# Fused clustered attention and channel mix: per-head transposes with long load runs, later weight loads, a later cluster step, and mix pieces kept for the end

## The chip, the cores and the metric

One core of one Trainium2 chip. Times are device microseconds of one execution. The span of a trace (first to last instruction) is about 2 us shorter than the execution's time. Engines: PE is TensorE (PEld its weight loads), DVE VectorE, ACT ScalarE, POOL GpSimd, SP the queue that issues most transfers.

## The reference, cut to what matters

```python
# q, k, v: (4 batches, 8 heads, 768 tokens, 64); 16 centroids per head
q_assign = argmax(q_n . c_n)   # cluster of each query, of each key
k_assign = argmax(k_n . c_n)
scores = where(q_assign == k_assign, scale * q @ k.T, -1e9)
attn_out = softmax(scores) @ v
# channel mix on x = attn_out as (4, 768, 512)
xk = mu_k*x + (1-mu_k)*x_prev ; xr likewise
out = sigmoid(xr @ w_r) * (max(xk @ w_k, 0)**2 @ w_v)
```

Of the kernel before, what the change touches and what calls it, by code (L numbers as in the profile page):

```python
# [8 lines left out]
F32 = mybir.dt.float32  # L9
# [7 lines left out]
def kernel(  # L17
# [24 lines left out]
    NG = 4  # L42
    GW = 2 * S // NG
    BIG = 32.0
    NWARM = 10

# [24 lines left out]
    def load_qk(n, eng_q, eng_k):  # L71
        b, j = divmod(n, NP)
        t = nat[n] = loadp.tile([128, 2, NCH, 2, D], F32, name="qk_nat")
        for i, (src, eng) in enumerate(((q, eng_q), (k, eng_k))):
            for h in range(2):
                eng.dma_start(t[:, i, :, h, :],
                              src[b, 2 * j + h].rearrange("(p c) d -> p c d", c=NCH))

    def load_v(n, eng):
        b, j = divmod(n, NP)  # L80
        t = vnat[n] = vloadp.tile([128, 2, NCH, D], F32, name="v_nat")
        for h in range(2):
            eng.dma_start(t[:, h, :, :], v[b, 2 * j + h].rearrange("(p c) d -> p c d", c=NCH))
# [4 lines left out]
    cblk = constp.tile([128, NP, 2 * C], F32)  # L88
# [14 lines left out]
    def krows(t):  # L103
        return slice(0, 64 + C) if t == 0 else slice(0, 128)

    def init_ring(i):
        nc.gpsimd.memset(augs[i][1][0:64, :], 0.0)
        nc.gpsimd.memset(vts[i][:, :, :, D:D + 1], 1.0)
        nc.gpsimd.memset(xts[i][:, 0, 0:1], 0.0)


    qkT = {}

    def trans(n, t3, eng=None):
        if t3 == 0:
            qkT[n] = qktp.tile([128, 2 * S], F32, name="qkT")
        ps = ps_w.tile([128, 512], F32, name="trps", tag="w")
        for i in range(4):
            qk, c = divmod(4 * t3 + i, NCH)
            nc.tensor.matmul(ps[:, i * 128:(i + 1) * 128], nat[n][:, qk, c, :, :], ident,  # L120
                             is_transpose=True, start=(i == 0), stop=(i == 3))
        cs = slice(t3 * 512, (t3 + 1) * 512)
        if eng is nc.scalar:
            nc.scalar.copy(qkT[n][:, cs], ps)
        else:
            nc.vector.tensor_copy(qkT[n][:, cs], ps)  # L126
        for t in range(2):
            rows = slice(64 * t, 64 * t + 64)
            nc.gpsimd.tensor_scalar(augs[n % NR][t][rows, cs], in0=qkT[n][rows, cs],  # L129
                                    scalar1=qk_scale, scalar2=1.0, op0=ALU.mult, op1=ALU.mult)  # L130
# [8 lines left out]
    def aff_mm(n):  # L139
        j = n % NP  # L140
        ps = ps_w.tile([128, GW], F32, name="affps", tag="w")
        for g in range(NG):
            nc.tensor.matmul(ps[32 * g:32 * g + 32, :], cblk[:, j, :], qkT[n][:, g * GW:(g + 1) * GW],  # L143
# [15 lines left out]
    def aff_back(n, engs):  # L159
# [3 lines left out]
        i = 0  # L163
        for t in range(2):
            o = 64 if t == 0 else 0
            for g in range(NG):
                engs[i % len(engs)].dma_start(augs[n % NR][t][o:o + C, g * GW:(g + 1) * GW],
                                              oht[32 * g + C * t:32 * g + C * t + C, :])
                i += 1
# [7 lines left out]
    def scores(t):  # L177
# [3 lines left out]
        rows = krows(tt)  # L181
# [129 lines left out]
    with tc.manual_schedule():  # L311
# [27 lines left out]
        cnt_ps = ps_o.tile([D, NP, 2, C], F32, name="cnt_ps", tag="out2")  # L339
        nc.tensor.transpose(cnt_ps.rearrange("d j t c -> d (j t c)"), cn_sb, ident)  # L340
        nc.vector.tensor_copy(cblk[0:64, :, 0:C], cnt_ps[:, :, 0, :])
        nc.vector.tensor_copy(cblk[64:128, :, C:2 * C], cnt_ps[:, :, 1, :])

        for n in range(2):
# [3 lines left out]
            load_qk(n + 2, nc.sync, nc.sync)  # L348
# [9 lines left out]
        nc.sync.dma_start(mu_k_sb, moe_mu_k.rearrange("(j p) -> p j", p=128))  # L358
        nc.sync.dma_start(mu_r_sb, moe_mu_r.rearrange("(j p) -> p j", p=128))

        def load_wk():
            nc.gpsimd.dma_start(w_k_sb, moe_w_k.rearrange("(j p) f -> p j f", p=128))

        def load_wv():
            nc.gpsimd.dma_start(w_v_sb, moe_w_v.rearrange("(i p) m -> p i m", p=128))

        def load_wr():
            nc.gpsimd.dma_start(w_r_sb, moe_w_r.rearrange("(j p) m -> p j m", p=128))

        def scale_wv():  # L370
            for i in range(NI):
                nc.gpsimd.tensor_scalar(w_v_sb[:, i, :], in0=w_v_sb[:, i, :], scalar1=0.5,
                                        scalar2=1.0, op0=ALU.mult, op1=ALU.mult)

        at(4, load_wk)
        at(16, load_wv)
        at(28, load_wr)
        at(50, scale_wv)

        W = 2 * NCH  # L380
        forced = {}
        for n in range(NPAIR):
            s = n * W
            if n + 2 < NPAIR:
                for t3 in range(3):
                    forced[s + t3] = lambda n=n, t3=t3: trans(n + 2, t3)
                if n + 4 < NPAIR:
                    at(s + 3, load_qk, n + 4, nc.sync, nc.sync)
                forced[s + 3] = lambda n=n: aff_mm(n + 2)
                at(s + 4, aff_max, n + 2)  # L390
                at(s + 5, aff_back, n + 2, [nc.sync])
            if n + 1 < NPAIR:
                at(s + 6, vcast, n + 1)
            if n + 2 < NPAIR:
                at(s + 7, load_v, n + 2, nc.sync)
# [24 lines left out]
        while t < NSTEP + NCH or queue or todo:  # L420
# [6 lines left out]
            elif queue and not (t < NSTEP and (B - 1) * H * NCH + W <= t and t % 6 == 5):  # L427
                queue.pop(0)()
# [31 lines left out]
```

## The kernel before: what the change touches

The mask is made by matmul: each head has a tile `aug` whose rows 0:64 are scaled q or k (transposed, tokens along columns) and whose next 16 rows are the one-hot cluster of each token. One matmul over the rows then gives score plus a large bonus where the clusters agree.

Work goes by pairs of heads (16 pairs) in 12 steps each, 192 steps in all. A step t issues, in this order on TensorE: `scores(t)` (one key chunk against 768 queries), `values(t-6)`, then either a forced task or one piece of the channel mix. ACT takes one exponential of 128x768 per step. Steps s to s+11 of pair n also prepare pair n+2:

```python
def load_qk(n, eng_q, eng_k):                    # 256 B runs, 4 DMAs a pair
    t = nat[n] = loadp.tile([128, 2, NCH, 2, D], F32, name="qk_nat")
    for i, (src, eng) in enumerate(((q, eng_q), (k, eng_k))):
        for h in range(2):
            eng.dma_start(t[:, i, :, h, :], src[b, 2*j + h].rearrange("(p c) d -> p c d", c=NCH))

def trans(n, t3, eng=None):                      # 4 transposes into one PSUM tile
    ...                                          # both heads of one token chunk
    nc.vector.tensor_copy(qkT[n][:, cs], ps)     # DVE: PSUM -> SBUF
    ...                                          # POOL: scaled copies into aug

def aff_mm(n):                                   # "the cluster matmul": 4 column groups of qkT
    for g in range(NG):
        nc.tensor.matmul(ps[32*g:32*g+32, :], cblk[:, j, :], qkT[n][:, g*GW:(g+1)*GW], ...)
    nc.vector.transpose(t1, ps)
# aff_max(n): DVE maximum and one-hot. aff_back(n): DVE transpose to oht, then 8 DMAs aug<-oht

for n in range(NPAIR):
    s = n * W                                    # W = 12
    forced[s + t3] = trans(n + 2, t3)            # t3 = 0, 1, 2
    at(s + 3, load_qk, n + 4, nc.sync, nc.sync)
    forced[s + 3] = aff_mm(n + 2)
    at(s + 4, aff_max, n + 2); at(s + 5, aff_back, n + 2, [nc.sync])
    ...
at(4, load_wk); at(16, load_wv); at(28, load_wr); at(50, scale_wv)     # whole weights, cast to bf16 on the way
while ...:
    scores(t); values(t - NCH)
    if t in forced: forced[t]()
    elif queue and not (t < NSTEP and (B-1)*H*NCH + W <= t and t % 6 == 5):
        queue.pop(0)()                           # one mix piece
```

Each batch puts 30 mix pieces (0.87 us of matmul each) on the queue when its last pair is done.

The softmax here doesn't subtract the row's maximum and nothing guards it: scores larger than these inputs give would overflow.

## Time and profile before

| | before |
|---|---|
| median of 3 runs | 297.51 us (295.93 to 297.65) |
| span of the trace | 296.0 us |
| TensorE busy | 268.1 us, 91% |
| ACT, DVE, POOL busy | 192.8, 179.4, 91.7 us |
| packets under 512 B | 54,368 of 65,661 |

How to read it: a busy share of 91% says that TensorE is the bound on average, and nothing about where the other 28 us are. The views that the prediction shows answer that. One more line of before matters below, from its list of waits (engine, line, what for: us in total, times, longest):

```profile
PEld affps L143 <- DVE qkT L126: 4.5, 16, 0.7
```

The weight loads of the cluster matmul wait for DVE's copy of the transposed block. Three of the 16 waits (1.4 us) belong to the first two pairs, which are prepared before the steps; the other 13 come one to a pair, in 13 of the 14 pairs that the steps prepare, 0.19 or 0.39 us each. It is a small row among some fifty, and I passed over it. One such wait in the timeline of before:

```profile
100.43 0.69 DVE L126 COPY qkT<-trps 128x512 f32<-128x512 f32 x1 [0.15 <-PE trps L120]
...
100.84 1.18 PE L143 MATMUL affps<-qkT,cblk 128*32 128x384 f32 x8
101.17 0.14 PEld L143 LDWEIGHTS affps<-qkT,cblk 128*32 128x32 f32 x4 [0.19 <-DVE qkT L126]
```

Four of the eight weight loads go at 100.84. The other four go at 101.17, just after DVE's copy ends (100.43 + 0.69 = 101.12). TensorE still counts as busy in between, since a recorded matmul of this group lasts 0.51 us.

### The profile page before, as it was taken

To read this page: it belongs to the slowest core of one execution; us is meant where nothing else is said; L and a number is where in the kernel's file an instruction comes from. 1 tells how busy PE (TensorE), PEld (TensorE's weight loads), DVE (VectorE), ACT (ScalarE), POOL (GpSimd) and SP (SyncE) were. 2 spreads that over 40 slices of the span, in tenths; PEclk is the share of its full clock that TensorE was granted. 3 is DMA by queue.
4 is the path that set the end of the run, shared out by engine and by line. 5 is a ranking of instruction groups with operands and counts; after the bars stand their busy time and mean duration, and the time that the engine had idled before them with its cause. 6 is when DMAs were issued, how large, how long until landed. Compare 5 with 4: busy or idle time off the path is not lost.

```text
span 296.0 us, 6426 instructions
## 1 busy us (share of the span) xinstructions
PE 268.1 (91%) x2479; PEld 165.7 (56%) x2507; DVE 179.4 (61%) x337; ACT 192.8 (65%) x268; POOL 91.7 (31%) x154
## 2 busy tenths in 40 slices
PE   6688949999899999999999999989999999869993
PEld 2345636656666656565666656555656555545441
DVE  2764744877967676655867677646766262765321
ACT  3048744877879776776779776666878866606320
POOL 2895607156970413324060605041241000000000
PEclk9979986999999999999999999999999999999999
DMA  8975995936633334435261506231302011110021
GB/s 159 221 164 89 185 188 134 196 76 151 167 107 80 84 87 144 104 132 142 63 151 50 123 15 187 74 112 44 97 6 64 2 71 38 71 38 0 35 108 71
DMA packets 65661, 29.81 MB, mean 101 GB/s; under 512 B 54368, under 2 KB 62048, under 8 KB 65632
## 3 DMA queue, kind: packets, MB, share of 16 engines
q1 hardware_dynamic: 61696, 26.32, 34.9%
q0 software_dynamic: 2096, 2.62, 5.9%
q10 hardware_dynamic: 1840, 0.48, 0.8%
q8 instruction: 20, 0.33, 0.5%
q14 instruction: 9, 0.07, 0.1%
HBM read 24.15 MB, written 6.29 MB: 103 GB/s over the span
## 4 chain that ended last, share of the span: by engine, by line
PE 71%; DVE 9%; ACT 8%; DMA 4%; POOL 3%; issue 3%; SPq 0%; DVEq 0%; ACTq 0%
PE psv L287 14%; PE st L184 10%; PE out L197 9%; PE psk L264 8%; PE trps L120 7%; ACT pt L187 7%; PE psr L276 7%; PE affps L143 5%; PE st L185 5%; PE psk L255 5%; POOL aug L129 3%; DMA aug<-oht 2%; DVE qkT L126 2%; DMA qk_nat<-in_q_dram 2%; PE xtps L217 1%
## 5 line engine op out<-in xcount | busy, mean ns | idle before, releaser
L187 ACT ACTIVATE pt<-st 128x768 bf16<-128x768 f32 x192 | 151.4, 809 | 60.4 <-PE st L185 50.6
L129 POOL TENSOR_SCALAR aug<-qkT 64x512 bf16<-64x512 f32 x96 | 59.4, 619 | 104.8 <-DVE qkT L126 98.9
L184 PE MATMUL st<-aug 80*128 80x512 bf16 (+1 forms) x192 | 74.3, 387 | 7.2 <-DMA aug<-oht 3.9
L197 PEld LDWEIGHTS <-pt 128*128 128x128 bf16 x1152 | 62.7, 98 | 30.3 <-ACT pt L187 4.6
L197 PE MATMUL out<-vt,pt 128*128 128x65 bf16 x1152 | 70.0, 194 | 2.9 <-ACT pt L187 2.3
L185 PE MATMUL st<-aug 80*128 80x256 bf16 (+1 forms) x192 | 52.7, 274 | 0.0
L287 PE MATMUL psv<-w_v_sb,k 128*128 128x512 bf16 x186 | 47.4, 378 | 0.3
L126 DVE COPY qkT<-trps 128x512 f32<-128x512 f32 x47 | 31.6, 702 | 19.3 <-PE trps L120 19.0
L269 ACT ACTIVATE kr<-psk 128x512 bf16<-128x512 f32 x48 | 28.7, 597 | 17.2 <-PE psk L264 13.2
L120 PE MATMUL trps<-ident,qk_nat 128*128 128x128 f32 x192 | 32.3, 294 | 6.0 <-DVE qkT L126 4.6
L291 DVE SCALAR_TENSOR_TENSOR out_sb<-tanh,psv 128x512 f32<-128x512 bf16 x24 | 16.5, 687 | 32.8 <-PE psv L287 26.7
L270 DVE TENSOR_TENSOR k<-kr 128x512 bf16<-128x512 bf16 x48 | 20.9, 436 | 24.7 <-ACT kr L269 24.7
L264 PE MATMUL psk<-xk,w_k_sb 128*128 128x512 bf16 x114 | 31.7, 378 | 3.8 <-DVE xk L240 3.1
L184 PEld LDWEIGHTS <-aug 80*128 80x128 bf16 (+1 forms) x192 | 19.0, 99 | 23.9 <-issue 10.8
L135 POOL CAST vt<-v_nat 128x384 bf16<-128x384 f32 x32 | 17.8, 580 | 31.3 <-DMA v_nat<-in_v_dram 30.5
L120 PEld LDWEIGHTS trps<-ident,qk_nat 128*128 128x128 f32 x192 | 21.6, 148 | 9.6 <-DVE qkT L126 5.9
L185 PEld LDWEIGHTS <-aug 80*128 80x128 bf16 (+1 forms) x192 | 19.1, 99 | 14.0 <-issue 4.4
L287 PEld LDWEIGHTS <-k 128*128 128x128 bf16 x192 | 16.3, 97 | 14.9 <-issue 1.3
L276 PE MATMUL psr<-w_r_sb,xr 128*128 128x512 bf16 x88 | 24.2, 378 | 0.4
L279 ACT ACTIVATE tanh<-psr 128x512 bf16<-128x512 f32 x24 | 14.3, 597 | 14.9 <-PE psr L276 14.7
L143 PE MATMUL affps<-qkT,cblk 128*32 128x384 f32 x128 | 19.7, 509 | 0.7 <-DVE qkT L126 0.5
L146 DVE STREAM_TRANSPOSE t<-affps 128x384 f32<-128x384 f32 x16 | 9.3, 583 | 15.8 <-PE affps L143 15.8
(48 smaller groups left out, 200.4 us busy)
## 6 DMA issues: line engine op xcount, KB each, us to landing
qk_nat<-in_q_dram SPq DMA_DIRECT2D x32, 192.0 KB, 3.9
v_nat<-in_v_dram SPq DMA_DIRECT2D x32, 192.0 KB, 2.7
out_dram<-out_sb SPq DMA_DIRECT2D x24, 256.0 KB, 2.3
qk_nat<-in_k_dram SPq DMA_DIRECT2D x30, 192.0 KB, 4.3
aug<-oht SPq DMA_DIRECT2D x124, 12.0 KB, 1.8
w_k_sb<-in_moe_w_k_dram POOLq DMA_DIRECT2D x1, 1024.0 KB, 9.2
w_v_sb<-in_moe_w_v_dram POOLq DMA_DIRECT2D x1, 1024.0 KB, 10.8
w_r_sb<-in_moe_w_r_dram POOLq DMA_DIRECT2D x1, 512.0 KB, 7.7
```

The source lines that it names most:

```text
L120: nc.tensor.matmul(ps[:, i * 128:(i + 1) * 128], nat[n][:, qk, c, :, :], ident, is_transpose=True, start=(i == 0), stop=(i == 3))
L126: nc.vector.tensor_copy(qkT[n][:, cs], ps)
L129: nc.gpsimd.tensor_scalar(augs[n % NR][t][rows, cs], in0=qkT[n][rows, cs], scalar1=qk_scale, scalar2=1.0, op0=ALU.mult, op1=ALU.mult)
L143: nc.tensor.matmul(ps[32 * g:32 * g + 32, :], cblk[:, j, :], qkT[n][:, g * GW:(g + 1) * GW], start=True, stop=True, tile_position=(0, 32 * g))
L184: nc.tensor.matmul(st[:, 0:512], kc, a[rows, 0:512], start=True, stop=True)
L185: nc.tensor.matmul(st[:, 512:S], kc, a[rows, 512:S], start=True, stop=True)
L187: nc.scalar.activation(pt, st, AF.Exp, bias=-BIG, scale=BIG)
L197: nc.tensor.matmul(o[:, qc, :], pts[bh * NCH + c][:, qc * 128:(qc + 1) * 128], vts[n % NR][:, tt, c, 0:D + 1], start=(c == 0), stop=(c == ...
L264: nc.tensor.matmul(ps, w_k_sb[:, j, ii * 128:(ii + 1) * 128], self.xk[:, j, 0:512], start=(j == 0), stop=(j == NJ - 1))
L269: nc.scalar.activation(kr, src, AF.Relu)
L276: nc.tensor.matmul(ps, self.xr[:, j, sl], w_r_sb[:, j, :], start=(j == 0), stop=(j == NJ - 1))
L287: nc.tensor.matmul(self.psvt, self.k2[:, i, sl], w_v_sb[:, i, :], start=(i == 0), stop=(i == NI - 1))
```

## The change

Its intent: longer load runs and fewer DMAs; no zero rows; transfers moved out of the crowded first 60 us; the cluster step one step away from the transposes that feed it; and some mix pieces kept for the gap at the end. The core of it (not shown: v too comes in one DMA a pair, and its load and its cast go one step later):

```diff
-        t = nat[n] = loadp.tile([128, 2, NCH, 2, D], F32, name="qk_nat")
+        t = nat[n] = loadp.tile([128, 2, 2, NCH * D], F32, name="qk_nat")
...
-            for h in range(2):
-                eng.dma_start(t[:, i, :, h, :], src[b, 2 * j + h].rearrange("(p c) d -> p c d", c=NCH))
+            eng.dma_start(t[:, i, :, :], src[b, 2 * j:2 * j + 2].rearrange("h (p c) d -> p h (c d)", c=NCH))
...
-        nc.gpsimd.memset(augs[i][1][0:64, :], 0.0)
...
-            nc.tensor.matmul(ps[:, ...], nat[n][:, qk, c, :, :], ident, is_transpose=True, ...)
+            nc.tensor.matmul(ps[:, ...], nat[n][:, g // 2, g % 2, c2 * 128:(c2 + 1) * 128], ident, is_transpose=True, ...)
...   # POOL: 8 copies of 64x384 a pair instead of 6 of 64x512; scores over 80 rows for both heads
-        at(4, load_wk) ; at(16, load_wv) ; at(28, load_wr) ; at(50, scale_wv)
+        at(6, load_mu)
+        for i in range(4):
+            at(22 + 6 * i, load_wk, i)
+            at(45 + 3 * i, load_wv, 2 * i)
+        for i in range(2):
+            at(57 + 3 * i, load_wr, 2 * i)
+        for i in range(NI):
+            at(56 + 2 * i, scale_wv, i)
...
-                    at(s + 3, load_qk, n + 4, nc.sync, nc.sync)
-                forced[s + 3] = lambda n=n: aff_mm(n + 2)
-                at(s + 4, aff_max, n + 2)
-                at(s + 5, aff_back, n + 2, [nc.sync])
+                at(s + 3, load_qk, n + 3, nc.sync, nc.sync)
+                forced[s + 4] = lambda n=n: aff_mm(n + 2)
+                at(s + 5, aff_max, n + 2)
+                at(s + 6, aff_back, n + 2, [nc.sync])
...
-            elif queue and not (t < NSTEP and (B - 1) * H * NCH + W <= t and t % 6 == 5):
+            elif queue and not (NSTEP - H * NCH // 2 < t < NSTEP + NCH - 1 and len(queue) <= HOLD):   # HOLD = 5
```

More of the change, by code (lines that the diff above doesn't have):

```diff
@@ L45 @@
     NWARM = 10
+    HOLD = 5
     qk_scale = (1.0 / (D ** 0.5) / BIG) ** 0.5
@@ L72, in load_qk @@
         b, j = divmod(n, NP)
-        t = nat[n] = loadp.tile([128, 2, NCH, 2, D], F32, name="qk_nat")
+        t = nat[n] = loadp.tile([128, 2, 2, NCH * D], F32, name="qk_nat")
         for i, (src, eng) in enumerate(((q, eng_q), (k, eng_k))):
-            for h in range(2):
-                eng.dma_start(t[:, i, :, h, :],
-                              src[b, 2 * j + h].rearrange("(p c) d -> p c d", c=NCH))
+            eng.dma_start(t[:, i, :, :],
+                          src[b, 2 * j:2 * j + 2].rearrange("h (p c) d -> p h (c d)", c=NCH))
     def load_v(n, eng):
@@ L81, in load_v @@
         t = vnat[n] = vloadp.tile([128, 2, NCH, D], F32, name="v_nat")
-        for h in range(2):
-            eng.dma_start(t[:, h, :, :], v[b, 2 * j + h].rearrange("(p c) d -> p c d", c=NCH))
+        eng.dma_start(t.rearrange("p h c d -> p h (c d)"),
+                      v[b, 2 * j:2 * j + 2].rearrange("h (p c) d -> p h (c d)", c=NCH))
     ident = constp.tile([128, 128], F32)
@@ L87 @@
     cn_sb = constp.tile([H * C, D], F32)
-    cblk = constp.tile([128, NP, 2 * C], F32)
+    cblk = constp.tile([128, H, 2, C], F32)
     mu_k_sb = constp.tile([128, NJ], F32)
@@ L101, with augv @@
         xts.append(constp.tile([128, NCH + 1, 128], BF16, name=f"xt{i}"))
-    def krows(t):
-        return slice(0, 64 + C) if t == 0 else slice(0, 128)
     def init_ring(i):
-        nc.gpsimd.memset(augs[i][1][0:64, :], 0.0)
         nc.gpsimd.memset(vts[i][:, :, :, D:D + 1], 1.0)
         nc.gpsimd.memset(xts[i][:, 0, 0:1], 0.0)
+    def augv(n, g):
+        a = augs[n % NR][g % 2].rearrange("p (q c r s) -> p q c r s", q=2, r=2, s=128)
+        return a[:, g // 2, :, :, :]
     qkT = {}
@@ L118, in trans @@
         for i in range(4):
-            qk, c = divmod(4 * t3 + i, NCH)
-            nc.tensor.matmul(ps[:, i * 128:(i + 1) * 128], nat[n][:, qk, c, :, :], ident,
+            g, c2 = divmod(4 * t3 + i, NCH // 2)
+            nc.tensor.matmul(ps[:, i * 128:(i + 1) * 128],
+                             nat[n][:, g // 2, g % 2, c2 * 128:(c2 + 1) * 128], ident,
                              is_transpose=True, start=(i == 0), stop=(i == 3))
@@ L126, in trans @@
             nc.vector.tensor_copy(qkT[n][:, cs], ps)
-        for t in range(2):
-            rows = slice(64 * t, 64 * t + 64)
-            nc.gpsimd.tensor_scalar(augs[n % NR][t][rows, cs], in0=qkT[n][rows, cs],
-                                    scalar1=qk_scale, scalar2=1.0, op0=ALU.mult, op1=ALU.mult)
+        for g in ((0,), (1,), (2, 3))[t3]:
+            for par in range(2):
+                src = qkT[n][64 * par:64 * par + 64, g * GW:(g + 1) * GW]
+                nc.gpsimd.tensor_scalar(augv(n, g)[0:64, :, par, :],
+                                        in0=src.rearrange("p (c s) -> p c s", s=128),
+                                        scalar1=qk_scale, scalar2=1.0, op0=ALU.mult, op1=ALU.mult)
     def vcast(n):
@@ L142, in aff_mm @@
         for g in range(NG):
-            nc.tensor.matmul(ps[32 * g:32 * g + 32, :], cblk[:, j, :], qkT[n][:, g * GW:(g + 1) * GW],
+            nc.tensor.matmul(ps[32 * g:32 * g + 32, :], cblk[:, 2 * j + g % 2, :, :],
+                             qkT[n][:, g * GW:(g + 1) * GW],
                              start=True, stop=True, tile_position=(0, 32 * g))
@@ L162, in aff_back @@
         nc.vector.transpose(oht, ohn)
-        i = 0
-        for t in range(2):
-            o = 64 if t == 0 else 0
-            for g in range(NG):
-                engs[i % len(engs)].dma_start(augs[n % NR][t][o:o + C, g * GW:(g + 1) * GW],
-                                              oht[32 * g + C * t:32 * g + C * t + C, :])
-                i += 1
+        for i, (g, par) in enumerate(((0, 0), (2, 0), (0, 1), (2, 1), (1, 0), (3, 0), (1, 1), (3, 1))):
+            r = 32 * g + C * par
+            engs[i % len(engs)].dma_start(augv(n, g)[64:64 + C, :, par, :],
+                                          oht[r:r + C, :].rearrange("p (c s) -> p c s", s=128))
     NSTEP = B * H * NCH
@@ L180, in scores @@
         a = augs[n % NR][tt]
-        rows = krows(tt)
+        rows = slice(0, 64 + C)
         st = ps_st.tile([128, S], F32, name="st")
@@ L338 @@
         nc.vector.tensor_scalar_mul(cn_sb, in0=cn_sb, scalar1=cn_rnorm)
-        cnt_ps = ps_o.tile([D, NP, 2, C], F32, name="cnt_ps", tag="out2")
-        nc.tensor.transpose(cnt_ps.rearrange("d j t c -> d (j t c)"), cn_sb, ident)
-        nc.vector.tensor_copy(cblk[0:64, :, 0:C], cnt_ps[:, :, 0, :])
-        nc.vector.tensor_copy(cblk[64:128, :, C:2 * C], cnt_ps[:, :, 1, :])
+        cnt_ps = ps_o.tile([D, H, C], F32, name="cnt_ps", tag="out2")
+        nc.tensor.transpose(cnt_ps.rearrange("d h c -> d (h c)"), cn_sb, ident)
+        nc.vector.tensor_copy(cblk[0:64, :, 0, :], cnt_ps)
+        nc.vector.tensor_copy(cblk[64:128, :, 1, :], cnt_ps)
         for n in range(2):
@@ L347 @@
             trans(n, 2)
-            load_qk(n + 2, nc.sync, nc.sync)
+            if n == 0:
+                load_qk(2, nc.sync, nc.sync)
             aff_mm(n)
@@ L357, with load_mu, load_wk, load_wv @@
         init_ring(2)
-        nc.sync.dma_start(mu_k_sb, moe_mu_k.rearrange("(j p) -> p j", p=128))
-        nc.sync.dma_start(mu_r_sb, moe_mu_r.rearrange("(j p) -> p j", p=128))
-        def load_wk():
-            nc.gpsimd.dma_start(w_k_sb, moe_w_k.rearrange("(j p) f -> p j f", p=128))
-        def load_wv():
-            nc.gpsimd.dma_start(w_v_sb, moe_w_v.rearrange("(i p) m -> p i m", p=128))
-        def load_wr():
-            nc.gpsimd.dma_start(w_r_sb, moe_w_r.rearrange("(j p) m -> p j m", p=128))
-        def scale_wv():
-            for i in range(NI):
-                nc.gpsimd.tensor_scalar(w_v_sb[:, i, :], in0=w_v_sb[:, i, :], scalar1=0.5,
-                                        scalar2=1.0, op0=ALU.mult, op1=ALU.mult)
-        at(4, load_wk)
-        at(16, load_wv)
-        at(28, load_wr)
-        at(50, scale_wv)
+        def load_mu():
+            nc.sync.dma_start(mu_k_sb, moe_mu_k.rearrange("(j p) -> p j", p=128))
+            nc.sync.dma_start(mu_r_sb, moe_mu_r.rearrange("(j p) -> p j", p=128))
+        def load_wk(j):
+            nc.gpsimd.dma_start(w_k_sb[:, j, :], moe_w_k.rearrange("(j p) f -> p j f", p=128)[:, j, :])
+        def load_wv(i):
+            nc.gpsimd.dma_start(w_v_sb[:, i:i + 2, :],
+                                moe_w_v.rearrange("(i p) m -> p i m", p=128)[:, i:i + 2, :])
+        def load_wr(j):
+            nc.gpsimd.dma_start(w_r_sb[:, j:j + 2, :],
+                                moe_w_r.rearrange("(j p) m -> p j m", p=128)[:, j:j + 2, :])
+        def scale_wv(i):
+            nc.gpsimd.tensor_scalar(w_v_sb[:, i, :], in0=w_v_sb[:, i, :], scalar1=0.5,
+                                    scalar2=1.0, op0=ALU.mult, op1=ALU.mult)
+        at(6, load_mu)
[6 more added lines that the diff above has]
+            at(56 + 2 * i, scale_wv, i)
         W = 2 * NCH
@@ L383 @@
             s = n * W
+            if n + 3 < NPAIR:
+                at(s + 3, load_qk, n + 3, nc.sync, nc.sync)
             if n + 2 < NPAIR:
@@ L386 @@
                     forced[s + t3] = lambda n=n, t3=t3: trans(n + 2, t3)
-                if n + 4 < NPAIR:
-                    at(s + 3, load_qk, n + 4, nc.sync, nc.sync)
-                forced[s + 3] = lambda n=n: aff_mm(n + 2)
-                at(s + 4, aff_max, n + 2)
-                at(s + 5, aff_back, n + 2, [nc.sync])
+                forced[s + 4] = lambda n=n: aff_mm(n + 2)
+                at(s + 5, aff_max, n + 2)
+                at(s + 6, aff_back, n + 2, [nc.sync])
+                at(s + 8, load_v, n + 2, nc.sync)
             if n + 1 < NPAIR:
-                at(s + 6, vcast, n + 1)
-            if n + 2 < NPAIR:
-                at(s + 7, load_v, n + 2, nc.sync)
+                at(s + 7, vcast, n + 1)
             at(s + W - 1, norm, 2 * n)
```

## The prediction

> **What bounds the kernel now.** I read the views in this order: the page's 40 slices, the table of windows, the chain that ended last, the timeline around its one long transfer, then the chain near the end. First the slices (each digit tenths of a slice of 7.4 us: busy share of TensorE, its granted clock, busy share of the DMA engines):
>
> ```profile
> PE   6688949999899999999999999989999999869993
> ...
> PEclk9979986999999999999999999999999999999999
> DMA  8975995936633334435261506231302011110021
> ```
>
> TensorE is at 9 nearly everywhere. The soft places are the first four slices, slices 6 and 7 (37 to 52 us, a 4 and a clock of 6) and slices 35 and 36 (about 255 to 270 us). The windows table separates these (columns: stretch, its length, busy us and count of PE, PEld, DVE, ACT, POOL, then clock, DMA share, GB/s):
>
> ```profile
> 43.00:60.00 17.00, 16.18 (x159) 11.68 (x160) 10.22 (x18) 11.31 (x15) 6.53 (x12) 0.82 0.80 171
> ...
> 100.90:117.00 16.10, 15.99 (x159) 10.21 (x162) 10.67 (x21) 11.66 (x17) 5.00 (x9) 1.00 0.42 114
> 249.40:265.40 16.00, 12.14 (x131) 7.32 (x131) 9.96 (x19) 6.65 (x9) 0.00 (x0) 1.00 0.13 50
> ```
>
> From 100.9 to 117.0 us one head pair (12 steps with eight pieces of the channel mix) takes 16.1 us with TensorE busy throughout, ACT 11.7, DVE 10.7, POOL 5.0, DMA at 0.42: TensorE-bound. The sum of the chain's own pieces agrees: 12 x (0.22 + 0.11 + 0.19) for scores and values, 8 x 0.87 mix, 3 x 0.47 transposes, 1.10 cluster matmul, 0.34 for the output transpose = 16.05 us. Nothing that shortens loads or moves them can help there. The other two stretches have holes.
>
> The cluster matmul (affps) comes once per pair, so its starts on the chain are a clock for the pairs:
>
> ```profile
> 32.19 1.13 PE affps L143 x6
> ...
> 49.48 0.97 PE affps L143 x8
> ...
> 60.48 1.13 PE affps L143 x6
> ...
> 71.64 1.10 PE affps L143 x6
> ```
>
> Before the mix begins (near 79 us) a pair takes 11.0 and 11.16 us: twelve exponentials of 0.809 us are 9.7, so this phase is bound by ACT, plus the steps in which transposes starve it. But the pair from 32.19 to 49.48 took 17.29 us. What took the time, on the chain:
>
> ```profile
> 35.16 0.59 SPq L167
> ...
> 35.79 7.19 DMA aug<-oht
> ...
> 43.02 0.61 PE st L184
> ```
>
> and in the timeline:
>
> ```profile
> 31.22 3.20 SPq L76 DMA_DIRECT2D qk_nat<-in_k_dram  x2
> 34.52 6.19 SPq L167 DMA_DIRECT2D aug<-oht  x8
> ...
> 43.02 0.61 PE L184 MATMUL st<-aug 80*128 80x512 bf16 x1 [3.92 <-DMA aug<-oht]
> 44.87 0.63 PE L184 MATMUL st<-aug 80*128 80x512 bf16 x1
> 50.91 0.38 PE L184 MATMUL st<-aug 80*128 80x512 bf16 x1
> ```
>
> The one-hot rows of the third pair were ready at about 25.5 us (DVE's transpose to oht runs 24.95 to 25.53), but their eight small copies start issuing only at 34.52: four q and k loads of 768 runs of 256 B each stand before them on SP, from 27.5 on, and they share the engines with the 1 MB w_k load issued at 24.57 (9.2 us to landing; two tiny mu loads took 9.0 and 7.7). The copies then need up to 7.2 us against a median of 1.8. TensorE stands still, and restarts slow: the same 128x512 score matmul takes 0.61 to 0.63 us until about 49 us and 0.38 after. Near the end:
>
> ```profile
> 260.82 0.69 DVE out_sb L291
> ...
> 261.76 0.57 DVE xn L210
> ...
> 264.34 1.03 DVE xk L240
> ...
> 265.41 0.38 PE psk L264
> ```
>
> After the last values matmuls (end 261.5) the last pair's normalise, transpose, shift chain runs through DVE until 265.4 while TensorE has only a transpose and three mix matmuls. From there the last batch's 30 mix pieces run back to back.
>
> **What the Trainium skill says.** "DMA: Bandwidth & Descriptors", section "Specifications", gives 512 B as the least transfer for line rate. The trace agrees: 54,368 of 65,661 packets are under 512 B, and while q and k come in 256 B runs the engines are full at about 215 to 220 GB/s; where the v load (1536 B runs) is in flight at 11 to 12 us they reach 349 to 386. The same page, "Issuing engines are not separate DMA queues", says that all issuing queues share the same 16 engines; the late one-hot copies beside w_k are that. "TensorE: Matmul & The Clock Gate", "Part 1: The HAM clock gate", puts an idle window of about 3.4 us before half clock; the 3.92 us wait and the 0.61 us matmuls after it agree. Its Part 2 ("Step-by-step") says that row count does not matter for a weight load; here 80-row and 128-row loads both take 97 to 101 ns, so cutting the odd head from 128 to 80 rows is worth nothing.
>
> **The change, part by part.**
>
> (1) Load runs of 1536 B, one DMA per pair of heads. Packets of q and k fall from 49,152 to 8,192. At the start, 786 KB (q and k of pair 0) at 220 GB/s is 3.6 us, at 360 GB/s 2.2 us; bulk flow began near 2.7 us, so both are there by about 5.5 us instead of 6.2 (q) and 7.4 (k). The warm-up matmuls and centroid transpose hold TensorE until 5.3 us, so I take 0.8 us of it.
>
> (2) No zeroing of the odd head's upper 64 rows. Three memsets of 1.37 us go. Two are on the early chain: the third runs 18.88 to 20.25 beside the DVE cast to identb, which takes 1.45 us there for 128x128, and a transpose then waits 1.12 us for DVE's copy behind it. I read this as the two engines holding each other up, and take 1.2 us. Start together: 2.0 us.
>
> (3) Weight loads split and later (w_k from step 22, not 4), the pair load one pair shorter ahead. In the early phase SP now issues: pair 1's one-hots from about 17 us (eight at 0.63 us, to 22), two qk loads (to 23.5), mu (to 25.7), then pair 2's one-hots, ready about 24, issued by 31 and landed by 34. They are needed at step 24. With step 3 near 19 us and 0.91 us per step that is 38 us. The stall goes: 17.29 - (11.0 + 11.16)/2 = 6.2 us, cold clock included.
>
> (4) Cluster step one step later. The three transpose steps (0.52 + 0.47 us each) and the cluster step (0.52 + 1.1) were adjacent, 4.6 us of TensorE against 3.2 of exponentials, with two score buffers to bridge. A plain step between them lets ACT keep fed: I estimate 0.1 us per pair over four ACT-bound pairs, 0.4 us. In the TensorE-bound part it is nothing.
>
> (5) The POOL copies are 128 instead of 96, 64x384 instead of 64x512. The mean of 619 ns should become about 510, so 8 x 0.51 against 6 x 0.62: 0.4 us more POOL per pair, at 5.0 of 16 us busy. Beside other work, 0.
>
> (6) Holding five mix pieces for the end. Counting pops: the third batch now finishes 25 pieces by step 182, holds from 183 to 196, and releases five at 197 to 201, into the gap at 261.5 to 265.4. Steps 183 to 191 then run at ACT's pace, 9 x 0.83 = 7.5 us, where TensorE needs 4.7. From after the cluster matmul of the last pair (step 160, 215.0 us) to 265.4 was 50.4 us. New sum: one more step with a piece 1.4, 22 steps at 1.39 plus two output transposes 31.3, held steps 7.5, last exponential 0.9, values 1.15, then three held pieces 2.6, transpose 0.5 and DVE's copy-shift chain 2.55, under which the other two pieces and three mix matmuls fit: 47.9. Gain 2.5 us. It also drops the skips at every sixth step, which had left the chain waiting on an exponential at head boundaries.
>
> Sum: 2.0 + 6.2 + 0.4 + 2.5 = 11.1 us off 297.5, 286.4 us.
>
> **The rivals.** (a) The stall is only moved: another wait takes its place, since weights (5 MB of reads) now land between steps 22 and 60 and DVE's one-hot transposes still wait for eight copy lanes. For it: the DMA share early is 0.92. Against it: the q and k transfers that fill it take about 0.6 of their time now, and the one-hots have about 4 us of slack at step 24 and more later. Then only 2.0 + 2.5 plus half the stall: about 290. (b) POOL becomes the bound in steps 22 to 70, with ten descriptor-writing DMA issues of 0.8 to 0.9 us, eight scalings of 0.87, 13% more copy time, and copies that now write other partitions than they read. If these copies cost double, POOL would need about 10 us of copies and 1.2 of casts per 11 us pair: no gain before 79 us, 293 or worse. The profile has no such shifted POOL copy; I give it 5%. (c) The held pieces give nothing, as starved steps 183 to 191 cost what the end gains: 289. (d) The loads were hidden anyway in the TensorE-bound middle: true, and already counted as zero.
>
> **Range and chances.** The stall is a measured wait and its removal has slack; start and end are sums of small terms, each perhaps 1.5 us wrong. Two rivals (a and c) reach 289 to 292; in the other direction, better pacing might give 3 us more. So 283.5 to 290.5, and 2% faster means below 291.6: 0.91 faster, 0.08 same, 0.01 slower.
>
> **What would show it.** Step 1: first transposes near 5.5 us, few packets under 512 B. Step 2: no long cast to identb. Step 3: cluster matmuls 11 us apart from the first to the fifth pair, no wait of PE for aug<-oht above 1 us, clock at 9 in slice 7, and the pair at 71.64 us now near 63. Step 5: 64x384 POOL copies near 0.51 us. Step 6: a stretch of ACT-paced steps without mix before the last values, and under 1.5 us of TensorE idling after them. The mix-phase pair should stay at 16.1 us; if it changes by more than 0.2 us, my account of the middle is wrong, and nine such pairs would move the total by more than any term here.

## More of the kernel before

The rounds of experiments ran on four chips, each with the kernel before beside it.

## The result, and the profile after

The changed kernel takes 281.67 us (median of 4 runs, 281.53 to 283.43) against 297.58 for the kernel before. The ratio is 0.948, 95% interval 0.942 to 0.954. (Ratios here are the mean time of one kernel's fast runs over that of the other's of the same rounds, so not quite the ratio of the medians.) Faster was right. The size was not: 15.9 us where 11.1 were predicted, and 281.67 lies below the range that began at 283.5.

The slices of the changed kernel, as for before, with the packet line:

```profile
PE   7678998997999999999999999999999999899994
PEclk9999999999999999999999999999999999999999
DMA  7425549669933216135602217135302102020021
...
DMA packets 28141, 29.80 MB, mean 107 GB/s; under 512 B 10704, under 2 KB 24528, under 8 KB 28112
```

The hole at 37 to 52 us is gone and the clock is full everywhere. The cluster matmuls on the chain:

```profile
30.24 0.78 PE affps L148 x8
...
40.59 0.78 PE affps L148 x8
...
51.28 0.78 PE affps L148 x8
...
61.66 0.83 PE affps L148 x8
```

The pairs before the mix now take 10.35, 10.69 and 10.38 us. The stall is gone, as predicted, but these are also faster than the 11.0 and 11.16 of before, and the matmul's own piece fell from about 1.10 to 0.78 us.

A sharper clock than these marks is the start of the exponential of each step, read from the traces (us from the span's start):

| step | before | after | gained so far |
|---|---|---|---|
| 0 | 17.21 | 15.30 | 1.9 |
| 6 | 24.56 | 21.63 | 2.9 |
| 30 | 52.42 | 42.61 | 9.8 |
| 54 | 74.72 | 63.68 | 11.0 |
| 78 | 105.42 | 94.99 | 10.4 |
| 150 | 203.11 | 190.88 | 12.2 |
| 180 | 242.32 | 231.58 | 10.7 |
| end | 296.0 | 279.7 | 16.4 |

(At step 180 the changed kernel has done more of the mix than the old one, hence the dip.) Between steps 6 and 30, where the stall was, it gained 6.9 us, near the 6.2 predicted. But it also gained where I had said nothing or little: 1.2 from 30 to 54, 1.8 from 78 to 150, and 4.2 after step 150, where I had 2.5. In the mix phase the cluster matmul's stretch of the chain shows what changed. Before:

```profile
100.72 0.19 PE out L197 x6
100.91 1.10 PE affps L143 x6
102.01 0.32 PE st L184
```

After:

```profile
107.76 0.19 PE out L200 x6
107.95 0.78 PE affps L148 x8
108.74 0.32 PE st L187
```

From the end of the values matmuls to the next scores it is 1.10 us before and 0.79 after, for eight matmul records each time (before, two of them are not on the chain). The list of waits agrees; what was 4.5 us, 16 times, is now 1.4 us, the three waits before the steps alone:

```profile
PEld affps L148 <- DVE qkT L129: 1.4, 3, 0.7
```

The end of the changed kernel, by windows (busy us of PE, PEld, DVE, ACT, POOL, then clock, DMA, GB/s):

```profile
215.00:235.00 20.00, 20.00 (x178) 11.43 (x176) 8.82 (x18) 14.58 (x21) 1.09 (x2) 1.00 0.17 60
235.00:243.50 8.50, 7.36 (x116) 5.47 (x115) 4.67 (x9) 7.05 (x10) 0.00 (x0) 1.00 0.09 33
243.50:249.50 6.00, 5.79 (x32) 2.62 (x29) 4.19 (x8) 0.60 (x1) 0.00 (x0) 1.00 0.12 46
```

Up to 235 us TensorE is full. From 235 to 243.5 are the steps without mix pieces, where ACT sets the pace. From 243.5 on the five pieces and the first matmuls of the last batch cover the DVE chain, with 0.2 us of 6.0 idle. From 235 us on that makes 1.35 us idle of 14.5, where the old kernel had 3.9 of 16.

### The profile page after: what moved, and what is told of

Read it like the earlier page. It is cut to its first block, busy times and chain, and to the rows that moved or that the text cites. A ratio compares the mean times of both kernels' runs of the same rounds, so it can differ in the third digit from the quotient of the medians.

```text
span 279.7 us, 6409 instructions
## 1 busy us (share of the span) xinstructions
PE 261.3 (93%) x2507; PEld 161.8 (58%) x2507; DVE 179.8 (64%) x337; ACT 192.4 (69%) x268; POOL 96.3 (34%) x190
## 4 chain that ended last, share of the span: by engine, by line
PE 74%; DVE 11%; ACT 8%; DMA 3%; issue 2%; ACTq 0%; DVEq 0%
PE psv L290 14%; PE st L187 11%; PE out L200 9%; PE psk L267 8%; PE trps L122 7%; PE psr L279 7%; ACT pt L190 7%; PE st L188 5%; PE affps L148 5%; PE psk L258 5%; DMA qk_nat<-in_k_dram 2%; DVE qkT L129 2%; DMA qk_nat<-in_q_dram 1%; DVE xk L243 1%; PE xtps L220 1%
## 5 line engine op out<-in xcount | busy, mean ns | idle before, releaser
L133 POOL TENSOR_SCALAR aug<-qkT 64x384 bf16<-64x384 f32 x128 | 66.2, 517 | 107.7 <-DVE qkT L129 100.6
L187 PE MATMUL st<-aug 80*128 80x512 bf16 x192 | 73.1, 381 | 2.5 <-ACT pt L190 1.9
L200 PE MATMUL out<-vt,pt 128*128 128x65 bf16 x1152 | 68.8, 193 | 2.3 <-ACT pt L190 2.0
L188 PE MATMUL st<-aug 80*128 80x256 bf16 x192 | 51.9, 270 | 0.0
L273 DVE TENSOR_TENSOR k<-kr 128x512 bf16<-128x512 bf16 x48 | 22.1, 459 | 25.7 <-ACT kr L272 25.7
L122 PE MATMUL trps<-ident,qk_nat 128*128 128x128 f32 x192 | 30.6, 282 | 5.7 <-DVE qkT L129 5.0
L187 PEld LDWEIGHTS <-aug 80*128 80x128 bf16 x192 | 18.8, 98 | 19.4 <-issue 11.9
L188 PEld LDWEIGHTS <-aug 80*128 80x128 bf16 x192 | 18.9, 99 | 12.5 <-issue 3.3
L122 PEld LDWEIGHTS trps<-ident,qk_nat 128*128 128x128 f32 x192 | 20.3, 141 | 8.9 <-DVE qkT L129 6.4
L140 POOL CAST vt<-v_nat 128x384 bf16<-128x384 f32 x32 | 16.4, 542 | 13.6 <-DMA v_nat<-in_v_dram 12.8
L213 DVE TENSOR_TENSOR xn<-out,rs 128x384 bf16<-128x384 f32 x32 | 17.8, 557 | 1.1
```

Source lines behind the costliest of these rows:

```text
L122: nc.tensor.matmul(ps[:, i * 128:(i + 1) * 128], nat[n][:, g // 2, g % 2, c2 * 128:(c2 + 1) * 128], ident, is_transpose=True, start=(i == ...
L133: nc.gpsimd.tensor_scalar(augv(n, g)[0:64, :, par, :], in0=src.rearrange("p (c s) -> p c s", s=128), scalar1=qk_scale, scalar2=1.0, op0=AL ...
L187: nc.tensor.matmul(st[:, 0:512], kc, a[rows, 0:512], start=True, stop=True)
L188: nc.tensor.matmul(st[:, 512:S], kc, a[rows, 512:S], start=True, stop=True)
L200: nc.tensor.matmul(o[:, qc, :], pts[bh * NCH + c][:, qc * 128:(qc + 1) * 128], vts[n % NR][:, tt, c, 0:D + 1], start=(c == 0), stop=(c == ...
L273: nc.vector.tensor_tensor(dst, kr, kr, op=ALU.mult)
```

## The experiments

My theory after the result: five parts, of which the cluster step's delay is worth several us and not 0.4, because it takes a wait of TensorE for DVE out of every pair. Rivals: the extra gain is the layout's (80 instead of 128 rows, less traffic), or the held pieces', or the stall's.

Each run's ratio is to the kernel before in the same round. The argument rests on the ratios beside each other and on the traces.

### One part undone at a time

**Cluster step back.**

```diff
-                forced[s + 4] = lambda n=n: aff_mm(n + 2)
-                at(s + 5, aff_max, n + 2)
-                at(s + 6, aff_back, n + 2, [nc.sync])
+                forced[s + 3] = lambda n=n: aff_mm(n + 2)
+                at(s + 4, aff_max, n + 2)
+                at(s + 5, aff_back, n + 2, [nc.sync])
```

> The changed kernel with only the cluster step moved back one step (cluster matmul in step s+3, maximum s+4, one-hot copies s+5). Theory 1: the gain that my prediction missed between steps 30 and 150 (3.0 us by the starts of the exponentials: 9.81 at step 30, 12.23 at step 150, plus 0.6 lost to mix order) comes from the cluster matmul no longer waiting for DVE's copy of the last transposed block. Then this kernel is slower than the changed one by 3 to 5 us (284.5 to 286.5), its cluster matmuls show about 1.10 us on the chain again, and a pair in the mix phase takes 0.3 us more. Theory 2: the gain is the new layout's (80 instead of 128 rows, larger load runs, less traffic): then within 1 us of the changed kernel.

Measured: 286.19 us (285.37 to 289.25), ratio 0.964 to before. In its trace it is later than the changed kernel by 0.7 us at step 6, 1.25 at 30, 2.2 at 54, 3.3 at 150 and 3.65 at the end. Its mix-phase pairs take 16.19 us (steps 66 to 138), the changed kernel's 15.93, the old kernel's 16.12. The wait is back:

```profile
PEld affps L148 <- DVE qkT L129: 5.1, 18, 0.7
```

Before the mix a pair takes 10.86, 11.19 and 10.86 us instead of 10.36, 10.69 and 10.38, so there the step costs 0.5 us a pair. Theory 1 holds, and the layout is out as its cause, since the layout did not change here.

**Old rule for the mix pieces.**

```diff
-            elif queue and not (NSTEP - H * NCH // 2 < t < NSTEP + NCH - 1 and len(queue) <= HOLD):
+            elif queue and not (t < NSTEP and (B - 1) * H * NCH + W <= t and t % 6 == 5):
```

> The changed kernel with the old rule for the mix pieces (skip every sixth step in the last batch, hold nothing). Theory 1: between step 150 and the end the changed kernel gained 4.1 us, of which holding is 3.5 to 4: this kernel is at 285 to 286. Theory 2 (the rival of my prediction, that held steps cost what the end gains, and the tail gain is something else): within 1.5 us of the changed kernel.

Measured: 285.94 us (285.12 to 288.93), ratio 0.9615; in the trace 0.4 us later than the changed kernel at step 150 and 3.66 at the end. The two rules do the same up to step 150, so holding is worth about 3.3 us in these traces, 4 by the ratios.

**Old weight loads** (whole w_k at step 4, w_v at 16, w_r at 28, scaling at 50, mu before step 0; the lines of the diff above, reversed).

> The changed kernel with the old weight loads: w_k whole at step 4, w_v at 16, w_r at 28, scaling at 50, mu before step 0. Theory 1: the stall needed both the 1 MB w_k load and the 256 B runs of q and k in front of the one-hot copies; with 1536 B runs the copies are late by 1 to 3 us at most: 282 to 285. Theory 2: the weight load alone made the stall: it comes back with 5 us or more, 287 or slower. Theory 3: it was the short runs alone: no change, within 1 us.

Measured: 291.37 us (290.55 to 292.36), ratio 0.978. The stall is back, and in another place. From its timeline:

```profile
22.93 0.93 POOL L367 DMA_DIRECT2D w_k_sb<-in_moe_w_k_dram  x1
...
23.91 0.45 SPq L76 DMA_DIRECT2D qk_nat<-in_q_dram  x1
...
33.11 1.11 PE L122 MATMUL trps<-ident,qk_nat 128*128 128x128 f32 x4 [6.91 <-DMA qk_nat<-in_q_dram]
```

The load of pair 3's q, issued 1 us after w_k, takes 9.2 us to land although it comes in long runs, and the first transposes wait 6.9 us for it, then run at half speed (1.11 us for four). Theory 2.

**Short runs** (wrong: q and k tokens are permuted).

```diff
-            eng.dma_start(t[:, i, :, :],
-                          src[b, 2 * j:2 * j + 2].rearrange("h (p c) d -> p h (c d)", c=NCH))
+            for h in range(2):
+                eng.dma_start(t[:, i, h, :].rearrange("p (c d) -> p c d", d=D),
+                              src[b, 2 * j + h].rearrange("(c p) d -> p c d", c=NCH))
```

> The changed kernel with q and k loaded in runs of 256 B again, two DMAs per q or k pair (tokens of q and k permuted, so the result is wrong on purpose; no instruction off the DMA queues changes). Theory 1: the start loses 1 to 1.5 us (first transposes at 6.2 to 6.5 us and k later), the stall stays away as the weights come later: 283 to 284.5. Theory 2 (short runs alone make the stall): 287 or slower with PE waiting for aug<-oht near step 24. Theory 3 (transfers were hidden): within 0.7 us.

Measured: 285.13 us (283.93 to 286.98), ratio 0.9575. By the exponentials it is 0.6 us later at step 0, level at step 6, and 2.2 later at step 42, with four short waits:

```profile
PE trps L123 <- DMA qk_nat<-in_q_dram: 1.8, 4, 0.5
```

None of the three expectations fits: the stall stayed away, the start lost nothing by step 6, yet 2.2 us went in pairs 2 and 3, when weights now load. Here q comes just in time; I put that down to the changed kernel loading it one pair later, and the run with old layout and three parts (below), with short runs but the old lead, agrees.

**Memsets put back** (rows that are overwritten or not read).

```diff
+        nc.gpsimd.memset(augs[i][1][64:128, :], 0.0)
```

> The changed kernel with the three memsets of 64x1536 on POOL put back (into rows that are overwritten or not read; still correct). Theory 1 (prediction, step 2): identb takes 1.4 us again behind the third memset and everything after it is 1.0 to 1.5 us later: 282.7 to 283.2. Theory 2: POOL has slack here and the start was held by something else: within 0.4 us of the changed kernel.

Measured: 283.05 us (282.68 to 283.23), ratio 0.949. The number is theory 1's, by luck: the cast to identb takes 0.50 us here, as in the changed kernel. The trace was 1.7 us later at the end, but already 2.0 at step 0, before the third memset. The unaltered changed kernel was 1.6 us later at step 0 in a later run, so at most the small rest can be the memsets'; see "A difference that is no kernel's" below.

### One part done alone on the kernel before

**Weights and mu later, nothing else** (the weight part of the diff on the old kernel).

> The kernel before with only the weight and mu loads of the changed kernel (split, from step 22 on; mu at step 6). Theory 1: the weight load at step 4 was what made the stall; the 256 B runs and the loads two pairs ahead only decided which wait showed it. Then the wait of PE for aug<-oht near step 24 falls below 1 us and the time to 290.5 to 292 (6 to 7 us off). Theory 2: the short runs of pair 4 in front of the one-hot copies are enough by themselves: 2 to 4 us of wait remain, 294 or slower.

Measured: 290.51 us (290.01 to 292.89), ratio 0.976. The exponentials run level with the old kernel to step 18 and are 6.3 us earlier at step 30; the end is 7.3 earlier. No wait of PE for aug<-oht is left in its list. So the stall was the weight load's: 256 B runs and loads two pairs ahead are all still there.

**Cluster step later, nothing else.**

> The kernel before with only the cluster step one step later. Theory 1 (the wait for DVE's copy, 0.3 us per pair in the mix phase and 0.5 in the ACT-bound pairs, independent of layout): 3 to 4 us off, 293.5 to 294.5, and the cluster matmuls take 0.78 us on the chain. Theory 2 (it pays only with the new layout, where the first two column groups are whole heads): under 1.5 us off.

Measured: 295.33 us (293.77 to 296.29), ratio 0.990, 1.9 us by the traces. That looks like theory 2. But the trace shows what ate the gain: it is 2.6 us ahead at step 18 (1.0 of it already at step 0, which the step cannot cause; the clock from 16 to 22 us is 1.00 here and 0.81 in the trace of before), then behind, because the stall was longer:

```profile
PE st L184 <- DMA aug<-oht: 8.9, 1, 8.9
```

against 3.9 in the trace of before. Whether the stall was longer because the one-hots now leave a step later, or by chance, this run does not show. After it, from step 30 to the end, it takes 240.4 us against 243.6, so 3.2 us come from the later pairs.

**Held pieces, nothing else.**

> The kernel before with only the new rule that holds five mix pieces for the end. Theory 1: the tail gain is the rule's alone: 3 to 4 us off, 293.5 to 294.5, all of it after step 180. Theory 2: it needs the other parts: under 1.5 us off.

Measured: 295.64 us (291.88 to 296.91), ratio 0.983 (0.974 to 0.993). Two of its four runs are slow, so the ratio is that of two runs. Its profile fell in the slow state, with a stall of 7.2 us that this change cannot cause, so only its end is of use: from step 150 it took 89.5 us against 92.9. The stall's length is thus not fixed. It may be part of the spread of the old kernel's runs (295.9 to 301.6 over all rounds), but that is not shown: a kernel without the stall spreads too (285.4 to 289.3 in four runs with the cluster step back).

### Do the parts add?

**All three schedule parts on the old layout**: weights later, cluster step later, five pieces held; 256 B runs, four DMAs, loads two pairs ahead, memsets and 128 rows stay.

> The kernel before with three parts of the change together: weights later, cluster step one step later, five pieces held; the layout, the 256 B runs, the loads two pairs ahead and the memsets stay old. Theory 1 (parts add; layout, runs and memsets are together worth 3 to 4 us, from the undone runs 2.3 and 1.7): 284.5 to 286. Theory 2 (the single runs from before, 0.9 and 1.9 us by the end of their traces for the other two, are the true sizes and the rest is the layout's): 287 to 289. Theory 3 (long runs and layout are worth nothing): under 283.

> The changed kernel unaltered, as the yardstick on the chip of the next three: 281.5 to 282, ratio to before 0.943 to 0.953.

Measured on the same chip, 6 runs each: 283.09 us (281.36 to 283.36, ratio 0.9508) for the three parts alone, 283.30 (281.67 to 284.07, ratio 0.9512) for the changed kernel. The yardstick itself missed its 281.5 to 282, though its ratio fell in the range expected. The three parts are just over the 283 of theory 3, but equal to the changed kernel beside them, which is theory 3 in substance and what I had thought least likely: with these parts in place, the long runs, the new layout, fewer DMAs and the missing memsets together show no gain (the runs of each kernel spread over 2 us or more). In traces with the same clock from 6 us on the changed kernel is 1.0 us ahead at step 0 (15.30 against 16.32), 0.5 at step 24, 0.7 at step 60, 0.1 at step 78, where the mix has begun, and at the end it is 279.7 against 279.6. By the ratios the parts add: alone they take off 2.4, 1.0 and 1.7% (each to within about 1), together 4.9.

**128 rows again** (memsets back, and `rows = slice(0, 64 + C) if tt == 0 else slice(0, 128)`).

> The changed kernel with the memsets put back and the odd head's scores over 128 rows again (48 rows of zeros, as before). Theory 1: rows cost nothing, so it equals the run with the memsets alone: 282.7 to 283.3. Theory 2 (the missed gain is the rows'): 285 or slower.

Measured: 282.63 us (280.73 to 282.75), ratio 0.949: no slower than the changed kernel beside it. Rows cost nothing, and this kernel has the memsets too, so they cost nothing either that these runs could show.

**Loads two pairs ahead again, weights late.**

```diff
-            if n + 3 < NPAIR:
-                at(s + 3, load_qk, n + 3, nc.sync, nc.sync)
+            if n + 4 < NPAIR:
+                at(s + 3, load_qk, n + 4, nc.sync, nc.sync)
```

> The changed kernel with q and k loaded two pairs ahead again, weights still late. Theory 1: with late weights the lead of the loads does not matter, within 1 us of the changed kernel. Theory 2: the earlier loads stand before the one-hots again and cost 1.5 us or more.

Measured: 281.57 us (281.10 to 283.27), ratio 0.948: theory 1, the lead makes no difference when the runs are long.

**Early weights with loads two pairs ahead.**

> The changed kernel with the old early weight loads and also the old pair loads two pairs ahead, so of the transfers only the run length (1536 B) and the DMA count differ from the kernel before. With early weights alone the stall moved to TensorE waiting 6.9 us for pair 3's q. Theory 1 (the early 1 MB weight load starves whatever is on the queues beside it): a wait of 3 us or more shows again, for q or for the one-hots, 285 or slower. Theory 2 (loads two pairs ahead give q enough lead, and long runs keep the one-hots from being late): the wait is under 1.5 us and the time within 2 us of the changed kernel.

Measured: 285.41 us (285.21 to 289.01), ratio 0.959. Theory 1 by the time, though milder. The trace is of the slowest of the four runs (289.01, at a mean clock of 0.97; the others took 285.2 to 285.5), so its waits may be longer than theirs. In it q has lead and the wait falls on v:

```profile
POOL vt L140 <- DMA v_nat<-in_v_dram: 11.6, 1, 11.6
...
PE out L200 <- POOL vt L140: 3.0, 1, 3.0
```

POOL sits 11.6 us for the v load beside the weights, and the values matmuls wait 3.0 us for POOL. With the same early weights, one-hots (old kernel), q (loads one pair ahead) or v (loads two pairs ahead) arrive late: whatever is in the queues beside them.

**A difference that is no kernel's.** Two traces of the identical changed kernel, the first and the repeat, from 10 to 16 us:

```profile
10.00:16.00 6.00, 3.88 (x26) 1.85 (x25) 4.77 (x9) 0.70 (x1) 5.37 (x13) 1.00 0.29 90
```

```profile
10.00:16.00 6.00, 3.87 (x20) 1.33 (x18) 4.27 (x7) 0.00 (x0) 5.37 (x13) 0.80 0.38 125
```

The granted clock is 1.00 in one and 0.80 in the other, and step 0 comes at 15.30 and 16.88. The trace of before has 0.90 here and 0.81 from 16 to 22 us; the one with the memsets has 0.78. So part of the 2.9 us that the two first traces differ at step 6 is this: with the clock at 1.00, the old layout with the three schedule parts reaches step 6 at 22.57, 0.9 us after the changed kernel. Up to 0.7 is the cluster step (the run with it undone), which leaves an estimated 1.3 for the clock.

### Tries at a faster version

**Transposes spread out**: steps s, s+2, s+4, cluster step s+6, maximum s+7, one-hots s+8, and v's load at s+9 instead of s+8.

> Try at a faster version: transposes of a pair in steps s, s+2, s+4 and the cluster step at s+6, one-hot copies at s+8. If the ACT-bound pairs before the mix still lose to TensorE doing three transpose steps in a row, they go from 10.4 to about 10.0 us: 1 to 2 us off, 280 to 280.7. If ACT is already fed: within 0.5 us of the changed kernel.

Measured: 286.54 us (285.04 to 287.23), ratio 0.961: slower. Its trace loses mostly between steps 30 and 60. I did not find the cause. From 42 to 80 us POOL waits 7.3 us for v's load, a row that the changed kernel lacks there, but no wait of TensorE for POOL's cast of v is listed.

**Steps without a piece spread evenly.**

```diff
-            elif queue and not (NSTEP - H * NCH // 2 < t < NSTEP + NCH - 1 and len(queue) <= HOLD):
+            elif queue and not (NSTEP - 32 < t < NSTEP and t % 6 in (1, 4) or NSTEP <= t < NSTEP + NCH - 1):
```

> Try at a faster version: instead of holding five pieces back at once (steps 183 to 196 without mix, ACT-bound, TensorE idle about 0.3 us a step), two steps of each six from 161 to 191 go without a piece, and six pieces are left for the end. If ACT and TensorE then balance over a head: 1.5 to 2.5 us off, 279.2 to 280.2. If a step without a piece costs the same wherever it stands: within 0.7 us.

Measured: 279.91 us (279.47 to 280.10), ratio 0.938 (0.931 to 0.945). Its traces run level with the changed kernel's to step 150 (190.54 against 190.88) and end at 277.6 against 279.7. From 235 us on:

```profile
235.00:243.50 8.50, 8.16 (x89) 4.96 (x89) 5.27 (x11) 4.08 (x6) 0.00 (x0) 1.00 0.16 62
```

TensorE is busy 8.16 of 8.5 us where the changed kernel had 7.36. This version beats both kernels, by 1.8 us against the changed one's first median. It was run at another time. The two intervals overlap (the changed kernel's is 0.942 to 0.954), but the stretch that the rule changes bears it out: from step 150 to the end it takes 87.05 us, and the changed kernel 88.80 and 89.52 in its two traces.

**Both tries.**

> Both tries together. If they act in different stretches, the gains add: 277.5 to 279.5; beats both kernels if under 281.

Measured: 286.63 us (285.69 to 287.13), ratio 0.960: the spread transposes lose more than the even steps gain.

## Why the prediction was wrong

The direction, the stall and most of the mechanisms were right. The failed step is (4), "Cluster step one step later", and in it the sentence "In the TensorE-bound part it is nothing", with its term of 0.4 us. It measured 3.65 us in the trace of the kernel with the step undone, 3.2 from step 30 on when done alone: 0.3 us a pair in the TensorE-bound part, and 0.5 in the ACT-bound pairs, where I had put 0.1. I had treated the step as a question of feeding ACT. It is also a question of TensorE's own order: in the old kernel the cluster matmul stands one step (0.5 us of matmuls) behind the last transposes, and DVE's copy of that block takes 0.70 us. The next scores start only after the last of the eight cluster matmuls (at 101.95 us in the pair shown above), so the difference, some 0.3 us, is lost in nearly every pair even while TensorE counts as busy. "TensorE busy throughout" at 15.99 of 16.1 us hid it, because the records of the first cluster matmuls (0.51 us each) reach over the wait of the others. My own sum of 16.05 us for a pair had the wait in it, as part of the "1.10 cluster matmul".

Point by point:

- (1) Long runs, 0.8 us. Right at the start and worthless at the end. First transposes came at 5.2 us (predicted 5.5) against 6.3; at equal clock step 0 is 1.0 us earlier; the end of the trace is not (279.7 against 279.6 without this part). That step 0 came 1.9 us earlier in the first two traces, near the 2.0 predicted for the start, is luck: 1.0 is left at equal clock. The runs are needed when the loads are issued later: undone alone they cost 2.3 us by the traces. The reading of 215 to 220 GB/s for 256 B runs was too narrow: the same view has 217 to 292 from 3 to 5 us, with every packet under 512 B and no v load issued yet.
- (2) Memsets, 1.2 us. Wrong as a fixed cost. In the trace of before the cast and the memset start together:

```profile
18.88 1.37 POOL L107 MEMSET aug<- 64x1536 bf16 x1
18.88 1.45 DVE L356 CAST identb<-ident 128x128 bf16<-128x128 f32 x1
```

and in the old layout with the three schedule parts, memset kept, at full clock, the cast comes first:

```profile
18.27 0.18 DVE L357 CAST identb<-ident 128x128 bf16<-128x128 f32 x1
19.00 1.37 POOL L108 MEMSET aug<- 64x1536 bf16 x1
```

So what I read as a fixed cost is an alignment that comes and goes. Of the five traces of the old layout two have it (before, and weights later alone), with 1.45 us for the cast; in the other three the cast comes 0.7 us earlier than the memset and takes 0.18. No run isolates what it costs where it occurs. Of the 2.9 us of early difference an estimated 1.3 was the granted clock.

- (3) Stall, 6.2 us. Right in kind, and near in size: 6.9 between steps 6 and 30 in the first two traces, 0.5 of it the cluster step; 6.2 there when the weights alone are moved, and 7.3 by the end. So close a hit has luck in it, as the stall's own length varies (3.9, 7.2 and 8.9 us of wait in three traces). I named the 256 B loads and w_k as joint causes; the runs show that the early weight loads suffice and the short loads alone do not. Rival (a), that the stall only moves, did not happen in the changed kernel, but it is what happens with early weights under the other two arrangements of the loads that I ran.
- (5) POOL: right. 64x384 copies took 517 ns (predicted 510), and rival (b) fell.
- (6) Held pieces, 2.5 us. Right mechanism, too small: from step 150 on, 3.3 us by the run with it undone and 3.4 done alone. The mis-sized term is the held steps with the last exponential, which I put at 8.4 us (7.5 and 0.9). On the chain they took 7.1, from the end of the last piece before the hold at 235.2 to the last exponential's end at 242.3. DVE's copy-shift chain took 3.1 where I had 2.55. Rival (c) fell.
- The test that I set for myself did its work: a mix-phase pair should stay at 16.1 us or "my account of the middle is wrong". The pair that I had timed (100.84 to 116.90 us in before) went from 16.06 to 15.76, the mean of it and the three after it from 16.15 to 15.85, and that pointed at the cluster step.
- One agreement with the skill was read too generally. The half clock did come with the 3.92 us wait that ends at 43 us, but before also has a half-clock stretch at about 15 to 18 us (mean clock 0.81 from 16 to 22), and TensorE's longest wait in the five us before it is 2.15 us.

Not settled: why the 1.0 us that the new layout is ahead at step 0 is lost again (0.5 between steps 12 and 18, the rest between 60 and 78), and why spreading the transposes loses.

## What to carry to other kernels

An engine shown as busy can still wait inside its busy time: compare the pieces of the chain with the sum of the instruction's own work, and try giving a consumer one more independent step's distance from the copy that feeds it. Read the small repeated rows of the wait list by their count (here 0.2 to 0.4 us in 13 pairs), not only by length. When several parts change together, run the parts alone from both ends: the part that the change was named for gave nothing here that the runs could show, and bulk loads moved to later steps (the first by 18) gave nearly half.

## What the Trainium skill lacked or had wrong

- "DMA: Bandwidth & Descriptors", "Issuing engines are not separate DMA queues", is right that queues share the engines, but no page gives the price of a casting weight load beside plain loads. Here, with early weights and loads two pairs ahead, from 20 to 45 us, the software queue's 2.09 MB (as written, cast to bf16) took 54.6% of the engines' time and the SP queue's 2.10 MB took 29.6% (counted as read, in f32, the first are 4.18 MB, which is about the same time per byte), and 12 KB copies took 5.8 us to land against a median of 1.8 in the changed kernel.
- The 512 B threshold of its "Specifications" section agreed with the rate (mostly about 220, at most 292 GB/s, against 349 to 386), and told little of the time: once the weights were late, six times fewer q and k packets changed the median by 0.2 us where the loads had two pairs' lead. With one pair's lead, undoing them cost 2.3.
- "TensorE: Matmul & The Clock Gate", "Part 1: The HAM clock gate", says that the warm-up varies from run to run, and bids us not to fit it. That holds (the first transposes took 271 ns each in one trace of the changed kernel and 421 in another) and matters when two single traces are compared. The clock also differs after the warm-up: from 10 to 16 us its mean was 1.00 and 0.80 in these two, and step 0 moved by 1.6 us.
